# A gated linear attention and an MLP mixer on one core: transposes of one batch element moved from the matrix engine to DMA, relu rows written whole, constants spread over engines, and a new written order

## The chip, the cores and the metric

The kernel runs on one core of a Trainium2 chip. A core has a matrix engine (PE), a vector engine (DVE), a scalar engine (ACT), a general engine (POOL) and an engine that here only issues transfers (SP). Each of them works through its own list of instructions in order and waits on semaphores for the others. Transfers (DMA) are issued by SP and POOL and carried out by 16 DMA engines; those issued by POOL are one queue of their own. The metric is the device time of one run in microseconds (us); lower is better.

## The reference

For each of 4 batch elements (b) and 8 heads a state of 48 x 48 is carried over 768 steps: it decays by a gate per row and takes up an outer product; the output is the query times the state. The outputs of the heads side by side are the rows x of 768 x 384, which go through a mixer over tokens and one over channels.

```python
f = 1.0 / (1.0 + np.exp(-f_logit))
for t in range(S):
    state = f[:, :, t, :, None] * state + np.einsum('bhd,bhe->bhde', k[:, :, t], v[:, :, t])
    y[:, :, t] = np.einsum('bhd,bhde->bhe', q[:, :, t], state)
...
xt = x.transpose(0, 2, 1)
h = np.maximum(xt @ w_tok1, 0.0) @ w_tok2
u = x + h.transpose(0, 2, 1)
h2 = np.maximum(u @ w_ch1, 0.0) @ w_ch2
return (u + h2).astype(np.float32)
```

## The kernel before

The 768 steps are cut into 6 chunks of 128 (c = 0 to 5). For a chunk, ACT makes the logarithms of the gates (`exp`, `ln`), DVE or POOL their low halves (`lo`, L374, L396), PE sums them with a triangle of ones (`sums`, L456, L457, L607, L610), ACT turns the sums into factors (`G`, `Gi`), DVE multiplies q and k with them (`gated`, L485, L629), PE transposes both (`turn`, L495, L636), and PE forms the `scores` (L408, L668), which DVE masks while it reads them from PSUM (`masked`, L536, L698). `parts` (L424, L657) are the outer products of a chunk. The state is carried from chunk to chunk by two DVE operations: `tsum` (L547, L728) adds the parts, and `state` (L549, L730) multiplies by the decay. `spread` (L344 on ACT, L348 on POOL) copies the state as bf16 into a block-diagonal tile for the next chunk, and `y` (L556, L560, L736) is the chunk's output, which leaves PSUM as `x_bf` and `x_nat`. Batch 0 works on its chunks in pairs (function `pair`).

The mixer of a batch element (function `mixer`) is: `tok1` (L750, 12 matmuls in two row tiles, rt 0 and 1) and a relu copy `h1T` (L757); `tok2` (L766) for six token tiles; `u` (L782) and its bf16 copy `u_bf`; the transposes of `u_bf` into `uT`; `ch1` (L819, 24 groups of 3 matmuls) with relu copies `zT`; `ch2` (L838, 6 token tiles with 12 matmuls each, in three blocks of four); `sum` (L844) and `store` (L848). `uT` is made in one of two ways. For batch elements in `UTURN` (2 and 3 before), SP issues two transposing transfers of three token tiles each (L795). For the others, PE makes 3 transposes of 128x128 for each of six token tiles (L804), and DVE or ACT copies each tile out of PSUM.

The queue of POOL holds, besides its arithmetic, all loads of q, k, v, of the gates f of batches 1 to 3 and of the weights (L264, L270); f of batch 0, the row `glast` of each chunk's decay (L476), some transposes and the stores are SP's.

What is done in which order on which engine isn't found by a scheduler at build time: every operation has a number in the order in which it is made in the code, and the string `ORDER` lists the numbers as they are to be issued. A letter behind a number chooses the engine (D for DVE, A for ACT, G for POOL) where an operation allows several, the digits behind a colon choose its PSUM banks, and `z3` stands for three filler matmuls of 512 columns on ones (L870), whose results are not used. Waits follow from the data; each engine takes its part of the list strictly in order. The constants (masks, zeros for padding, ones) are made by `memset` (L277) and `once` at the head of the list, before all on DVE but one.

Of the kernel before, what the change touches and what calls it, by code (L numbers as in the profile page):

```python
# [18 lines left out]
UTURN = (2, 3)  # L19
# [8 lines left out]
POOLED = ()  # L28
LOADS0F = [('f', (0, 2)), ('f', (2, 4)), ('f', (4, 6))]
# [5 lines left out]
32 33 10 5 34 15 21 9 8 22 13 11 0 1 36 24 27 2 49 3 6 35 12 14 20 23 25 26 50 28 7 37 51 52D 54 53D 38 17 z13 105:0  # L35
55 39 19 58 56D 100:1 42 57D 107 29 102 40 z1 137:2 30 106 104 142:3 101 110 43 108 59 103 109 31 119:0:1 18 143 60G
114:4 139 125 111:5 4 61D 144 115 112 41 141 180:0 113A 116D 127G 147 44 138 130 151:4 146 117:5:6 140 181 152 62 121
175:2 126A 131 120 118:5:1 177 176 122 z2 148:6 153A z1 149 123 132G 156:1:2 45 145 182 124:5:4 162 183 178 150A 133G
184 179 47 z3 186:0 163 128A 134 169 155:6:1 135A 185 46 187 159 129A 189:2 188A 208:3 160 190 165G 154:1:5 64 191A
216:6 157 209 67 158 136A z3 193:2:5 164A 217 66 198 192:4:1 170 z1 161:0:2 63 196 195 197 z6 166 194:4 171A 172G 341  # L40
173 200 199:5:1 167A 201 174D 202A 203G 204 210 347 218 71 205D 206 338 211 219 207D 342 212 220 339 213 343G 221 214D
215A 222A 223D 232:3 344 168D 228:4 340G 233 348 229 240 234 224:0 345 241 68 230 244 225 243A 236 252:6 226 242A
250:7 349G 237 245 253D 251A 360:5 231 239A 248:6 346G 256:7 362 249D 368:4 238D 257A 272:6 65 246A 235 280:2 273A 227
254:3 363 396:7 281D 404:0 255A 364 247D 258:6 370 259A 262:2 74 361 270:1 263D 350 69 266:6 369 16 284:2 73 399 264:5
285D 400 260:3 72 271D 265A 302:2 267A 373 300:1 353 70 365 371 374:6 301D 354 48 366:5 372 375D 303A 306:1 261A 75
286:2 398 307D 296:3 367D 287A 355G 378:1 397 377:2 407 381 376:7 76 389 408 304:4 380 276:1 78 305A 388 274:7 405 387
383G 282:4 382A 351 79 278:2 379 283A 294:6 406 401 77 288:5 352D 295A 290:0 275A 409 402:6 277A 289D 291A 384:7 403D
292:1 386A 410:0 279A 390 293D 393:5 297A 392G 298:2 80 395A 411D 433:3 299A 394D 412:1 391G 436 413:4 385D 81 414:5
435 437 416 268:2 434 471:7 417 464:3 269A 424 441:1 472 328:2 425 313:0 415 418 323:4 426 420G 438 421:6 419G 324 82
427 423A 442 430:5 422A 84 325 432D 431A 465 443 439:6 83 326 473 444 314 440A 88 449:4 428A 445:1 452 86 429A 315  # L50
446D 466 453 447:4 448:5 454A 455G 451 467 85 329 450 474 318:4 87 459 456:6 460 319 457A 458D 461:5 316 468 475 462D
308:6 589 356 469 476 320 590 470D 586 477D 330 463D 587 493:7 598 321 481:5 588G 592 331 478:3 595 484:4 479 89 490:0
596 309 482 591D 483A 333:1 485 599 310 494 480A 486G 491 334 495G 597D 604:5 97 600D 487:3 605 496:0 500:7 606 94
498:4 497D 612:2 501D 492A 335 499D 614 488 593 510:4 609 615 530:3 594G 336 613 506:7 311 522:0 511A 93 601 617 610:2
523A 508:4 90 607 640:6 509D 608 518:0 641 91 611D 616 618:4 507A 516:1 531D 489A 92 519A 619D 648:5 504:3 517A 502:7
98 505D 643 620:0 503D 621:1 823 644 622:3 632 96 642 524:7 649 623 534:1 95 650 624 526:6 544:2 357 535D 527A 514:0
631 824 528:6 525A 515D 820 628:4 645 536:7 529A 630D 677:1 545A 646:6 625 537A 546:2 633 651 627G 647D 678 358 532:7
652 629A 653 540:0 626A 533D 547A 656:3 634 541A 658:4 680 654:2 661 659 602 636G 512:0 681 635A 99 520:7 679 662
637:5 513A 660 603G 554:1 655A 670 550:0 682 664G 556:6 639A 663G 521A 657:4 638A 693:3 668 555A 665:7 685:5 832 669
715:2 557 686 551D 687 683:4 667D 666A 708:5 688 829 538:0 671 821 558 539D 673A 822G 833 674:7 696 559 826 689:0 359  # L60
684A 716 548:3 690D 542:6 675D 676A 838:1 825D 543A 709 692:7 672A 549D 691:6 830 704 710 827 571:3 695 561:7 694 711
717 703 845:6 566:4 847 697 839 699G 700:0 846 831G 718 567 701D 841 848 562 698G 842 840 849 572 835 843 332 702D
705:1 327 552:6 706A 707D 317 712 719 828D 553A 844 576:0 720 713 573 721A 714D 872:2 574 722:5 875 737:6 850 731:3
876 738 734:1 851 563 723 739A 735 724A 577 732 736A 581:1 564 733G 834D 728:3 741 582 729 725:7 730A 568 726 874 583
727A 569 836 740 854:3 584 853:4:7 852:5:6 864 879:1 578 855 880 881 784:4 863 873 780:6 579 882 766:2 857 877 772:0
858G 865 907:1 878 773A 770:7 785A 774:0 767A 771D 760:4 859A 312 781D 910 786:7 322 761D 869:6 866 787A 762:4 856
868A 867G 775A 756:2 884 860:5 757A 744:0 885 908 778:7 745D 862A 886:2:3 837D 861A 911 888:0 763A 776:5 883 891 909
890 782:4 777A 892 750:1 779A 900 894G 768:5 783D 751A 893G 752:0 871A 889 914:4 753A 912 742:1 916 870D 895:0 769A
748:3 915 913 746:5 749A 887:4:6 897A 747D 921:7 337 758:2 898 575 788:5 899 759A 936:6 896A 810:3 789D 743A 917 943:0
904:5 919:1:4 918 905D 944 811 922 945 901 937 570 812 924 903A 902G 923 580 938 946 925 764:7 927G 754:1 765A 800:4  # L70
906A 755D 926A 920:5:7 939 932 795:1 931 928:2 801 929D 933:7 947 940 934A 935D 802 948 941 796 949A 942A 790:0 930A
959:6 965:5 950:2 966 962:7 797 967A 963 815:5 960 964G 951 961A 791 952A 969 816 956:6 953:7 957 805:2 565 798 958G
792 954 813 806 955G 803 817 968 793 807 1000:3 1004:7 1016:1 1005A 994:6 1001A 1017D 1002:7 818 1010:1 1003A 819
1014:5 1011D 794 986:7 1015D 799 976:1 987A 585 974:5 996:7 975D 982:3 808 980:5 995D 983A 809 1008:2 981D 560 998:6
977D 984:3 997D 999A 988:1 985A 972:6 989D 978:3 1009D 973A 970:1 1012:2 971A 990:6 1013D 1048:1 1006:7 991A 979A
1033:5 1007A 1038:3 1043:6 1034 1039 1023:7 1018:0 992:2 1049 1044 993A 1050 1040 1051 1052 1028:2 1041 1045 1042 1024
804 1035 814 1025 1036 1029 1046 1026 1047 1019 1027 1030 1037 1020 1031 1032 1021 1022
# [68 lines left out]
def kernel(  # L146
# [126 lines left out]
    def once(name, engine, fn, make, own, need=()):  # L273
        return add(("once", name), engine, fn, make=make, need=need, kind=("fix", own, own))
# [629 lines left out]
```

## Time and profile before

| what | us |
|---|---|
| median of 3 timed runs (lowest, highest) | 173.81 (173.71, 174.67) |
| span of the profiled execution, first to last instruction | 172.8 |
| PE busy | 164.4 |
| DVE busy | 129.1 |
| ACT busy | 109.7 |
| POOL busy | 78.0 |

The profiled execution's own time is known as its span; what lies around the span (start and end of the program) is taken as the difference between the median and the span, 173.81 - 172.8 = 1.0 us. Busy times are unions of an engine's instructions. The page cuts the span into 40 slices of 4.3 us and gives a digit of busy share for each; "PEclk" is the clock that PE was granted, "DMA" the mean busy share of the DMA engines. A row of the groups names source line, engine, operation, result and operand, shape and count, then busy time, mean duration in ns, and the idle time just before with its releaser. A row of the chain gives start, length, engine, tile and line of a piece of the work that ended last.

### The profile page before, as it was taken

The numbers are of one execution on the slowest core, as the hardware profiler recorded it, in microseconds if no ns is written. First come the engines' busy times: TensorE is split into PE (matmuls) and PEld (weight loads), VectorE is DVE, ScalarE is ACT, GpSimd is POOL, SyncE is SP. The second block draws the span as 40 slices with busy tenths as digits, with TensorE's granted clock in tenths as the row PEclk, the third lists the DMA queues.
The fourth block names the chain that finished last, engine by engine and source line by source line (L and its number), as shares of the span: only waits on it lengthen the run. The fifth ranks groups of instructions, "written<-read, shape, count | busy, mean of one in ns | idle before, by whom it ended". The sixth has DMA issues, their size and how long they took to land.

```text
span 172.8 us, 4455 instructions
## 1 busy us (share of the span) xinstructions
PE 164.4 (95%) x1758; PEld 103.6 (60%) x1762; DVE 129.1 (75%) x287; ACT 109.7 (64%) x246; POOL 78.0 (45%) x102
## 2 busy tenths in 40 slices
PE   6889998999999999999999999999999999999991
PEld 2465755566676666676667566666565656656660
DVE  6989996978997789989969859887786355581132
ACT  3997938999893656799999685479933430444100
POOL 2999846998566893799663330010101012000000
PEclk9999999999999999999999999999999999999999
DMA  5999999999997998999999995638155006250054
GB/s 146 217 169 175 246 210 210 157 122 129 197 134 154 182 109 197 133 60 114 108 135 69 63 141 135 144 81 157 32 154 154 1 19 163 89 188 0 2 200 168
DMA packets 89573, 22.74 MB, mean 132 GB/s; under 512 B 82288, under 2 KB 88736, under 8 KB 89552
## 3 DMA queue, kind: packets, MB, share of 16 engines
q0 software_dynamic: 69600, 13.77, 91.7%
q1 hardware_dynamic: 19952, 8.69, 19.6%
q8 instruction: 14, 0.23, 0.6%
q14 instruction: 7, 0.06, 0.1%
HBM read 25.17 MB, written 4.72 MB: 173 GB/s over the span
## 4 chain that ended last, share of the span: by engine, by line
PE 75%; ACT 8%; DVE 5%; issue 1%; DVEq 0%
PE ps L838 26%; PE ps L819 23%; PE ps L750 4%; PE ps L766 4%; PE ps L408 3%; ACT zT L352 2%; PE ps L495 2%; PE ps L456 2%; PE ps L560 2%; PE ps L457 1%; ACT L L367 1%; PE ps L870 1%; PE ps L424 1%; PE ps L804 1%; PE ps L556 1%
## 5 line engine op out<-in xcount | busy, mean ns | idle before, releaser
L838 PE MATMUL ps<-w_ch,zT 128*128 128x384 bf16 (+2 forms) x300 | 52.9, 319 | 0.0
L819 PE MATMUL ps<-uT,w_ch 128*128 128x384 bf16 x288 | 52.4, 326 | 0.3 <-ACT GG L468 0.2
L352 ACT ACTIVATE zT<-ps 128x384 bf16<-128x384 f32 x61 | 28.2, 493 | 19.6 <-PE ps L819 14.6
L838 PEld LDWEIGHTS <-zT 128*128 128x128 bf16 x300 | 28.4, 98 | 17.4 <-issue 0.2
L819 PEld LDWEIGHTS <-w_ch 128*128 128x128 bf16 x288 | 26.9, 97 | 17.0 <-issue 0.7
L354 DVE TENSOR_SCALAR zT<-ps 128x384 bf16<-128x384 f32 x35 | 18.9, 554 | 10.4 <-PE ps L819 8.9
L536 DVE TENSOR_TENSOR AmT<-ps,tri_bf 128x512 bf16<-128x512 f32 x36 | 23.1, 683 | 2.3 <-PE ps L408 2.1
L348 POOL CAST state_bd<-state 48x192 bf16<-48x192 f32 x24 | 9.0, 376 | 34.6 <-DVE state L549 22.2
L844 DVE TENSOR_TENSOR x_nat<-x_nat,ps 128x384 f32<-128x384 f32 (+2 forms) x25 | 12.8, 534 | 10.3 <-PE ps L838 9.8
L264 POOL DMA_DIRECT2D qk_sb<-in_q_dram x16 | 15.9, 1000 | 0.8 <-issue 0.8
L264 POOL DMA_DIRECT2D qk_sb<-in_k_dram x16 | 15.7, 983 | 0.3 <-issue 0.3
L264 POOL DMA_DIRECT2D v_sb<-in_v_dram x16 | 15.7, 983 | 0.1
L782 DVE TENSOR_TENSOR x_nat<-x_nat,ps 128x384 f32<-128x384 f32 x21 | 10.8, 549 | 4.2 <-PE ps L766 4.1
L750 PE MATMUL ps<-x_bf,w_tok 128*128 128x384 bf16 x48 | 13.2, 326 | 0.3 <-DVE zT L698 0.2
L348 POOL CAST u_bf<-x_nat 128x384 bf16<-128x384 f32 x6 | 3.0, 506 | 20.7 <-DVE x_nat L782 20.7
L374 POOL TENSOR_TENSOR Llo<-L 128x384 bf16<-128x384 f32 x10 | 8.2, 826 | 6.4 <-ACT L L367 6.3
L485 DVE TENSOR_TENSOR qk<-qk_sb,GG 128x768 bf16<-128x768 bf16 x18 | 9.9, 555 | 1.4 <-ACT GG L468 1.4
L870 PE MATMUL ps<-x_nat 128*128 128x512 bf16 x26 | 8.7, 460 | 2.0 <-DVE x_nat L279 1.5
L466 ACT ACTIVATE GG<-ps 128x384 bf16<-128x384 f32 x18 | 8.7, 492 | 2.5 <-PE ps L457 2.3
L344 ACT ACTIVATE x_bf<-ps 128x384 bf16<-128x384 f32 x13 | 6.5, 499 | 5.9 <-PE ps L560 5.0
L766 PE MATMUL ps<-h1T,w_tok 128*128 128x384 bf16 x48 | 9.4, 326 | 0.8 <-ACT h1T L352 0.6
L468 ACT ACTIVATE GG<-ps 128x384 bf16<-128x384 f32 x18 | 8.9, 492 | 1.8 <-PE ps L457 1.6
(96 smaller groups left out, 266.4 us busy)
## 6 DMA issues: line engine op xcount, KB each, us to landing
out_dram<-x_nat SPq DMA_DIRECT2D x23, 192.0 KB, 2.2
f_sb<-in_f_logit_dram POOLq DMA_DIRECT2D x3, 1152.0 KB, 11.1
f_sb<-in_f_logit_dram SPq DMA_DIRECT2D x3, 384.0 KB, 4.2
w_ch<-in_moe_w_ch_dram POOLq DMA_DIRECT2D x2, 576.0 KB, 13.2
qk_sb<-in_q_dram POOLq DMA_DIRECT2D x12, 96.0 KB, 6.6
qk_sb<-in_k_dram POOLq DMA_DIRECT2D x12, 96.0 KB, 5.6
v_sb<-in_v_dram POOLq DMA_DIRECT2D x12, 96.0 KB, 4.5
w_ch<-in_moe_w_ch_dram POOLq DMA_DIRECT2D x1, 1152.0 KB, 10.0
```

What stands on the lines that cost most here:

```text
L264: lambda eng=eng, into=into, of=of: eng.dma_start(out=into, in_=of),
L348: nc.gpsimd.tensor_copy(out_, in_)
L352: nc.scalar.activation(out_, in_, AF.Relu, bias=0.0, scale=1.0)
L354: nc.vector.tensor_scalar(out_, in_, 0.0, None, ALU.max)
L536: add(("masked", b, c, p), DVE, lambda half=half, made=made: nc.vector.tensor_tensor(half, made(), tb4, ALU.mult), need=["tri_bf"], make=[ ...
L750: add(("tok1", b, rt, kt), PE, lambda rt=rt, kt=kt, pm=pm: nc.tensor.matmul(banks[pm.at][:, 0:DM], lhsT=w_tok1[:, kt, rt * 128:(rt + 1) * ...
L766: nc.tensor.matmul(banks[pm.at][:, 0:DM], lhsT=w_tok2[:, kt, tt * 128:(tt + 1) * 128], rhs=h1T[:, kt, :], start=(kt == 0 and not held), st ...
L782: nc.vector.tensor_tensor(to, un, banks[pm.at][:, 0:DM], ALU.add)
L819: nc.tensor.matmul(banks[pm.at][:, 0:384].rearrange("p (n t) -> p n t", t=128), lhsT=w[:, kt, c0:c0 + 128], rhs=uT[:, rows3, kt, :], start ...
L838: nc.tensor.matmul(banks[pm.at][:, 0:n1 - n0], lhsT=zT[:, kt, tt * 128:(tt + 1) * 128], rhs=w_ch2[:, kt, n0:n1], start=(kt == 0), stop=(kt ...
L844: add(("sum", b, tt, n0), DVE, lambda un=un, pm=pm, n=n1 - n0: nc.vector.tensor_tensor(un, un, banks[pm.at][:, 0:n], ALU.add), make=[("x_n ...
L870: nc.tensor.matmul(banks[NBANK - 1][0:rows, 0:cols], lhsT=steady[:, 0:rows], rhs=steady[:, 0:cols], start=True, stop=True)
```

## The change

Five things are changed.

1. `UTURN` becomes (1, 2, 3): the 18 PE transposes of batch 1's `u_bf` and their six copies out of PSUM give way to two transposing transfers that SP issues.
2. `h1T` of batch 0 is copied in two whole rows (384 columns), not in four halves.
3. The constants may be made by DVE or POOL (`memset`) and by DVE or ACT (`copied`). In the new list 11 of the memsets are POOL's and 2 copies are ACT's.
4. The `state` multiplication of a chunk may run on POOL; in the new list 11 of 20 do, three of them in batch 0.
5. `ORDER` is a new list for all engines. It has 23 filler matmuls where the old one had 30 (13 of them at the head in both), other engines for some copies, other PSUM banks, and another order of the loads.

The diff, without the two lists and with the moved helper `copy_on` left out:

```diff
-UTURN = (2, 3)
+UTURN = (1, 2, 3)
...
+HALVES = False
+STATES = (DVE, POOL,)
...
     def memset(name, tl, value, make, own):
-        once(name, DVE, lambda: nc.vector.memset(tl, value), make, own)
+        op = once(name, (DVE, POOL), None, make, own)
+        op.fn = lambda: (nc.gpsimd if op.engine == POOL else nc.vector).memset(tl, value)
+
+    def copied(name, out_, in_, make, own, need):
+        op = once(name, (DVE, ACT), None, make, own, need)
+        op.fn = lambda: copy_on(op.engine, out_, in_)
...
-    once("ident0", DVE, lambda: nc.vector.tensor_copy(ident[:, 0:1], tri_bf[:, 0:1]), ["ident"], 70, ["tri_bf"])
+    copied("ident0", ident[:, 0:1], tri_bf[:, 0:1], ["ident"], 70, ["tri_bf"])
...
-            once(f"inc2{n}", DVE, lambda rows=rows: nc.vector.tensor_copy(inc2[rows, rows], tri_bf[rows, rows]), ["inc2"], 130,
-                 ["tri_bf"])
...
+            copied(f"inc2{n}", inc2[rows, rows], tri_bf[rows, rows], ["inc2"], 130, ["tri_bf"])
+            copied(f"pmask0{n}", pmask[0][rows], tri_bf[rows, rows].unsqueeze(2).broadcast_to((64, 64, 2)), [("pmask", 0)], 200,
+                   ["tri_bf"])
...
-                add(("state", b, c), DVE, lambda: nc.vector.tensor_tensor(state, tsum, gb, ALU.mult),
-                    need=["tsum", ("glast", g4)], make=["state"], kind=small)
+                decayed(b, c, gb, ("glast", g4))
...
+    def decayed(b, c, gb, key):
+        op = add(("state", b, c), STATES, None, need=["tsum", key], make=["state"], kind=("el", HP * D, True, 1))
+        op.fn = lambda: (nc.gpsimd if op.engine == POOL else nc.vector).tensor_tensor(state, tsum, gb, ALU.mult)
...
-            half = DM // 2 if b == 0 else DM
+            half = DM // 2 if b == 0 and HALVES else DM
```

What the new list does at the places that the prediction speaks of:

- **Head.** POOL makes tri, one zero tile and five paddings before its first load; DVE has fewer constants ahead of its first `lo`, and all six `lo` of batch 0 are DVE's.
- **Loads.** POOL issues the gates f of batch 1 ahead of v of the last chunk pair and of the token weights; the set of transfers ahead of `w_tok2` stays the same.
- **First mixer.** All 12 `tok1` of batch 0 stand behind the last `y`. The six of rt 0 and one of rt 1 come first, the other five of rt 1 last. Of the twelve `tok2` matmuls, the first four need only rt 0. `h1T` of rt 0 is DVE's and of rt 1 is ACT's. One `sums` of batch 1 (two matmuls of 384) now stands in the attention of batch 0.
- **Batch 1's `uT`.** The last of the first three `u_bf` hangs on the `tok2` of token tile 2, behind which PE has six blocks of four `ch2` matmuls and three `tok2` pairs until the first `ch1` of batch 1. On POOL's queue f of batch 2 and seven loads of its v, q and k stand ahead of that point; only one `state` among them waits for anything.

More of the change, by code (lines that the diff above doesn't have):

```diff
@@ L40 @@
[L40 to L54, printed above, removed]
@@ L75 @@
[L75 to L77 removed]
+0G 18G 1 12D 2 11D 24A 21D 20D 32 27D 5G 23A 49 33 8G 17G 50 51 29D 22D 26D 54 10D 13G 7D 14D 3D 25D 6G 36 34 55 28 35
+37 30D 52D 58 39 z13 53D 9G 105:0 100:1 106 15D 56D 101 57D 142:2 102 103 38 40 108 137:1 107 31D 110 109 59 143 19G 144
@@ L271, in load_w, with copy_on @@
             make=[name], kind=("load", 900, 1024, size))
+    def copy_on(eng, out_, in_):
+        if eng == ACT:
+            nc.scalar.activation(out_, in_, AF.Copy, bias=0.0, scale=1.0)
+        elif eng == DVE:
+            nc.vector.tensor_copy(out_, in_)
+        else:
+            nc.gpsimd.tensor_copy(out_, in_)
     def once(name, engine, fn, make, own, need=()):
@@ L340, in blk @@
         return ap3.rearrange("t (hp par) dd -> t hp (par dd)", par=2)
-    def copy_on(eng, out_, in_):
-        if eng == ACT:
-            nc.scalar.activation(out_, in_, AF.Copy, bias=0.0, scale=1.0)
-        elif eng == DVE:
-            nc.vector.tensor_copy(out_, in_)
-        else:
-            nc.gpsimd.tensor_copy(out_, in_)
     def relu(eng, out_, in_):
@@ L729, in pair @@
                         need=["state"], make=["tsum"], bank=p_d[k], kind=small)
-                    add(("state", 0, c), DVE, lambda gb=gb: nc.vector.tensor_tensor(state, tsum, gb, ALU.mult),
-                        need=["tsum", ("gpair", i2)], make=["state"], kind=small)
+                    decayed(0, c, gb, ("gpair", i2))
                 spread(0, c)
```

72 lines of the change are left out of this document (42 added, 30 removed).

## The prediction

> **What bounds the kernel now.** I read the page's first two parts, then busy time by stretch, then the chain of waits around the seam between the first two stretches.
>
> ```profile
> span 172.8 us, 4455 instructions
> ...
> PE 164.4 (95%) x1758; PEld 103.6 (60%) x1762; DVE 129.1 (75%) x287; ACT 109.7 (64%) x246; POOL 78.0 (45%) x102
> ...
> PE   6889998999999999999999999999999999999991
> DVE  6989996978997789989969859887786355581132
> ...
> DMA  5999999999997998999999995638155006250054
> ```
>
> PE looks like the bound everywhere, but fillers count as busy. The stretches below tell more; the columns are stretch, length, then busy time and count of PE, weight loads, DVE, ACT and POOL.
>
> ```profile
> 5.90:28.80 22.90, 20.80 (x437) 13.79 (x439) 20.47 (x50) 17.74 (x38) 18.29 (x24) 1.00 1.54 197
> 28.80:32.70 3.90, 3.12 (x22) 1.70 (x21) 2.77 (x8) 3.44 (x10) 3.53 (x6) 1.00 1.67 183
> 32.70:169.30 136.60, 136.01 (x1291) 86.39 (x1289) 101.24 (x208) 85.66 (x197) 53.39 (x67) 1.00 1.07 117
> ```
>
> From 32.7 us on PE is busy 136.0 of 136.6 us: there every PE instruction costs its time, and every wait of PE is new time. In the attention of batch 0 (5.9 to 28.8 us) DVE has 20.5 of 22.9 us with its waits for PE and transfers in the rest, and PE's 20.8 us hold 17 fillers: there DVE leads. So the sum has two parts: when the first `tok2` can stream, and what PE must do after it.
>
> ```profile
> 28.21 0.98 PE ps L750 x5
> 29.21 0.37 DVE h1T L354
> 29.61 0.56 ACT h1T L352 x2
> 30.19 0.37 DVE h1T L354
> 30.60 1.46 PE ps L766 x8
> ```
>
> The seam: `tok1` ends at 29.19, four half copies of `h1T` follow one another, and `tok2` streams only from 30.60 (two of its matmuls went before). 1.4 us for 0.33 us of PE work.
>
> **The change part by part. The front.** DVE's work there, by group (result and operand, count, then busy us and mean ns):
>
> ```profile
> L698 DVE TENSOR_TENSOR zT<-ps,x_nat 128x512 bf16<-128x512 f32 x12 | 7.7, 682 | 0.4 <-PE ps L668 0.4
> ...
> L396 DVE TENSOR_TENSOR Llo<-L 128x384 bf16<-128x384 f32 x5 | 2.5, 528 | 0.0
> L730 DVE TENSOR_TENSOR state<-tsum,gpair 128x192 f32<-128x192 f32 x4 | 1.4, 354 | 0.2
> ...
> L323 DVE COPY x_nat<-x_nat 64x64 bf16<-64x64 bf16 x2 | 1.0, 492 | 0.1
> ...
> L277 DVE MEMSET state_bd<- 128x192 uint32 x2 | 0.4, 218 | 0.2
> ...
> L321 DVE COPY x_nat<-x_nat 128x128 bf16<-128x128 bf16 x1 | 0.3, 345 | 0.0
> ```
>
> And five rows of the timeline (start, length, engine, line, operation):
>
> ```profile
> 5.14 0.94 ACT L383 ACTIVATE L<-f_sb 128x384 f32<-128x384 f32 x2
> ...
> 5.94 0.50 DVE L396 TENSOR_TENSOR Llo<-L 128x384 bf16<-128x384 f32 x1
> ...
> 10.97 0.83 POOL L396 TENSOR_TENSOR Llo<-L 128x384 bf16<-128x384 f32 x1 [0.23 <-ACT L L383]
> ...
> 11.07 0.78 DVE L323 COPY x_nat<-x_nat 64x64 bf16<-64x64 bf16 x1
> ...
> 27.26 1.54 DVE L346 CAST x_bf<-ps 128x384 bf16<-128x384 f32 x3
> ```
>
> Between the first `lo` and the last `x_bf`, the new list takes from DVE: two zero tiles (2 x 0.218), the copy of L321 (0.345) and one of L323 (two in 0.98 us, one of them 0.78, so the other 0.20), which now stand before the first `lo` or on POOL: 1.0 us; and three of the four L730 (3 x 0.354 = 1.06). It adds the sixth `lo` (0.53). Masks and `x_bf` keep their number (12 and 3). Net: 1.0 + 1.06 - 0.53 = 1.5 us; 2.1, if the other L323 falls from 0.78 to 0.20. The first `lo` started at 5.94, behind DVE's constants; its logarithm, the first of two in 0.94 us from 5.14 on, is done by about 5.6. With fewer constants ahead `lo` can start then: 0.3 us more. So the last `x_bf` of batch 0 comes about 1.8 us sooner, at 27.0 instead of 28.8 (27.26 + 1.54). From there, six `tok1` remain by the new list instead of two: four more at 0.163 us (four matmuls as wide in 0.65 us, L838 below) are 0.65 us back. The seam itself shrinks: rt 0's relu (one row of 0.55 us on DVE) lies under the five last `tok1`, the first four `tok2` (0.65 us) lie over rt 1's relu on ACT (0.5 us), and some 0.3 us of wait is left instead of 1.1: 0.8 us won. Together 1.8 - 0.65 + 0.8 = 2.0 us (1.95): where `tok2` streamed from 30.60 with two done, as good as 30.3, it streams from about 28.3.
>
> Fillers stand only where PE waits, so the seven that go are inside this sum and not added to it. Transfers allow it: the set ahead of `w_tok2` is the same as before, POOL's queue is full from the start, and `w_tok2`, issued at 16.7, landed 10.4 us later, at 27.0.
>
> ```profile
> L270 POOL DMA_DIRECT2D w_tok<-in_moe_w_tok_dram x1: 713/713/713, 16.7 to 16.7; - x1
> ...
> DMA to landing us min/median/max: 10.4/10.4/10.4
> ```
>
> Nearly all `tok2` need it at once, so the front can win at most 3.3 us (30.3 - 27.0); at the low end it wins nothing, if ACT (17.7 us busy, and with gates of batch 1 moved ahead of its `h1T`) takes the lead. I take 2.0.
>
> The moved constants on POOL: no row of before has a POOL memset of such a size. From below, nothing; from above, 0.83 us each, the row of POOL's `lo` of 384 columns. They stand before its first load, in time in which POOL had waited for DVE's triangle; each us by which they outlast it moves all loads and that floor by as much, which the range holds. The `state` on POOL: bounded by 0.35 (DVE's row) and 0.83 (twice the columns); about 0.45, 0.1 us more per step of the state's chain, hidden behind DVE's masks.
>
> **After the first `tok2`.** Rows of the chain for what leaves PE, and for the time of batch 1's `tok2`:
>
> ```profile
> 35.11 0.17 PE ps L456
> 35.28 0.16 PE ps L457
> ...
> 66.27 1.62 PE ps L766 x10
> ...
> 71.16 0.50 PE ps L804 x9
> 71.99 0.65 PE ps L838 x4
> ```
>
> 18 transposes at 0.50 / 9 = 55.6 ns are 1.0 us, all on the bound. One `sums` (0.33 us) now runs in the front, where PE has room: 0.3 us. The six copies of `uT` leave DVE and ACT, which are not the bound there: 0. `ch1` and `ch2` keep their counts.
>
> What comes instead is a wait. PE's list has, between the `tok2` of token tile 2 of batch 1 and the first `ch1` on its `uT`, six blocks of `ch2` (0.65) and three pairs of `tok2` (0.33): 4.9 us. In that time the chain `u` on DVE, `u_bf` on ACT, transfer must end:
>
> ```profile
> L782 DVE TENSOR_TENSOR x_nat<-x_nat,ps 128x384 f32<-128x384 f32 x21 | 10.8, 549 | 4.2 <-PE ps L766 4.1
> ...
> L344 ACT ACTIVATE u_bf<-x_nat 128x384 bf16<-128x384 f32 x12 | 6.1, 522 | 6.0 <-DVE x_nat L782 6.0
> ...
> uT<-u_bf SPq DMA_TRANSPOSE x4, 2.8
> ...
> f_sb<-in_f_logit_dram POOLq DMA_DIRECT2D x3, 1152.0 KB, 11.1
> ...
> w_ch<-in_moe_w_ch_dram POOLq DMA_DIRECT2D x1, 1152.0 KB, 10.0
> ```
>
> 0.55 + 0.52 + 2.8 = 3.9 us: hidden, with 1.0 us to spare. But the four transfers behind the 2.8 ran after 108 us, in slices of the DMA line with 6 tenths or less. Those of batch 1 fall with its `tok2` at about 66 us, in slices of 8 and 9 tenths, and POOL's list has f of batch 2 (11.1 us to land) and seven loads ahead of them. How a transposing transfer fares there no row tells. The nearest is SP's small transfer of `glast`, by its landing in two stretches, 100 to 106 us and 35 to 44 us:
>
> ```profile
> DMA to landing us min/median/max: 2.0/2.0/2.7
> ...
> DMA to landing us min/median/max: 3.5/4.3/6.1
> ```
>
> It takes 1.5 to 4.1 us more among loads, 2.3 in the middle. For `uT` that gives 4.3 to 6.9 us, against 3.8 that are hidden: a wait of 0.5 to 3.1 us, and in proportion (2.8 x 6.1 / 2.0 = 8.5) up to 4.7; from below, 0. I take the least busy end plus some, 0.9 us, since by its list POOL has only loads of q, k and v left in its queue then, as at the 3.5. The second transfer has about the same slack, and a wait for the first gives it more. For `glast` of batch 1, which now stands nearer to its `state`, and for `w_ch2` (10.0 us to land, issued later), I add 0.2 us; 0 to 2 is open.
>
> **Sum.** -2.0 (front) - 1.0 (transposes) - 0.3 (`sums`) + 0.9 + 0.2 (waits) = -2.2 us. The tail after the last `ch2` keeps its shape. The profiled span of 172.8 becomes 170.6; with the 1.0 us around the span that lie between it and the median of 173.8, **171.6 us**.
>
> **Rivals.** First, slower: **the transposes land late among the loads.** Each is a transfer of many small pieces that shares the 16 DMA engines with POOL's full queue. If `uT` takes three times its 2.8 us, as `glast` did at its worst, PE stands 4.7 us instead of 0.9: -2.2 - 0.9 + 4.7 = +1.6, 175.4 us. It decides from a landing of some 7 us on, where the wait eats the 3.3 us won and no gain is left. For it: the 8 and 9 of the DMA line at 66 us and the 6.1. Against it: the 3.5, and a queue that should have drained to small loads by then.
>
> Second, **the front doesn't get shorter**: ACT, which gets four operations of batch 1 ahead of rt 1's `h1T`, or the landing of `w_tok1` and `w_tok2`, takes DVE's place. Then -1.3 + 1.1 = -0.2: 173.6 us.
>
> Third, **POOL's new arithmetic holds DVE up.** The two copies of L323 speak for it: 0.20 us the one, 0.78 the other, which ran beside POOL's `lo` (10.97 to 11.80). If two of the three POOL `state` of the front each block DVE for their 0.45 us, 0.9 of the 2.0 us is lost: 172.5. Against it: much of DVE's work there are masks that read PSUM (L698, 7.7 of 20.5 us), and the state's product comes right behind a `tsum`, with masks next in DVE's list. The Trainium skill, page "SBUF — State Buffer", section "Who interferes with whom", has a rule that speaks against this part of the change: DVE and POOL share one pair of ports as an exclusive lock; a DVE copy in its fast modes, or a DVE operation with two SBUF inputs, and a POOL operation that reads SBUF keep each other out for a whole instruction. By that rule, the 0.78 agrees.
>
> That the change doesn't do what it says is excluded: the new list has six PE `ut` and six transfers, as said.
>
> **How the numbers follow.** Forecast 0.52 (its own range 169.8 to 172.9: -4.0, with the front at 2.7 and no waits, to -0.9, with the front at 1.0 and 1.4 of waits); late transposes 0.21; front unchanged 0.15; POOL against DVE 0.12. The measurement can tell about 0.5% from no change, 0.9 us: under 172.9 is faster, over 174.7 slower. Forecast and POOL's rival are faster (0.64), the unchanged front is the same (0.15), the late transposes are slower (0.21). For 8 in 10 the range runs from 169.8 up to 175.2, which leaves out about half of the late transposes and a little below.
>
> **What would show it.** Right: the first `tok2` streams by 28.3 us; DVE's busy time between the first `lo` and the last `x_bf` down by 1.5 to 2 us; L804 gone from the stretch after 60 us, and the first `ch1` of batch 1 waiting for a transfer by about 1 us. Wrong: that wait at 3 us or more and SP's transposes landing after over 6; a first `tok2` at 30; waits of PE for `glast`'s `state` or for `w_ch2`.

## The result and the profile after

The changed kernel takes 183.8 us (median of four runs, 181.5 to 185.9) where the kernel before takes 173.9 on the same chip: slower, ratio 1.045 [1.037, 1.053]. The ratio leaves out the two slowest of the four runs; the medians of all runs stand at 1.057. The profiled execution is the slowest of the four, 185.9 us with a span of 184.1; its clock was 0.969 on the mean, that of the fastest 0.991.

The page of the changed kernel, first two parts, rows as in the prediction's first fence:

```profile
span 184.1 us, 4400 instructions
...
PE 166.1 (90%) x1734; PEld 104.2 (57%) x1737; DVE 127.3 (69%) x267; ACT 105.3 (57%) x232; POOL 90.5 (49%) x128
...
PE   6999689895969999879679999999999999999992
...
PEclk9999999996996999999978999999999999999998
```

PE has new holes (the digits below 9 up to the 21st slice of 4.6 us, some 97 us), and the clock dips three times. From 98 us on PE runs as before. What ends the holes is in the chain of waits (start, length, piece):

```profile
37.85 4.46 DMA glast<-grow
...
42.44 0.36 DVE state L548
...
43.57 1.12 PE ps L825 x3
...
48.90 5.66 DMA glast<-grow
...
54.69 0.52 POOL state L576
...
55.65 0.34 PE ps L756
...
74.26 5.01 DMA uT<-u_bf
...
79.31 0.82 PE ps L825 x4
...
84.42 7.45 DMA glast<-grow
...
91.99 0.06 DVE state L548
...
93.00 0.65 PE ps L825 x3
```

Three of the four holes end with a gate row, `glast`: 2 KB that SP moves from `grow` so that the state of a chunk can be multiplied. It takes 4.5 to 7.5 us to land; PE's first instruction behind each comes 1.1 to 1.3 us after the landing, through DVE or POOL. The third hole ends with the first transposing transfer of batch 1. The changed kernel by stretch (length, busy time and count of PE, PEld, DVE, ACT and POOL, then granted clock, DMA share and GB/s):

```profile
43.60:46.30 2.70, 2.70 (x19) 1.60 (x19) 1.58 (x3) 1.45 (x4) 2.70 (x4) 0.50 0.88 46
...
55.60:62.00 6.40, 6.36 (x49) 4.00 (x50) 5.12 (x10) 3.34 (x8) 5.18 (x7) 0.73 1.54 80
...
93.00:98.00 5.00, 5.00 (x22) 2.46 (x22) 4.42 (x9) 2.73 (x7) 4.05 (x4) 0.66 0.45 25
98.00:180.40 82.40, 81.79 (x759) 52.12 (x756) 54.54 (x108) 40.06 (x91) 20.32 (x32) 1.00 0.74 103
```

Behind each gate row's hole PE runs for some time at a lower clock: busy, and yet half as fast. If the gaps between the starts of PE's groups of matmuls beyond their pitch are added up over the trace (no view shows this sum), PE lost 7.5 us before and 21.2 after, 13.7 more; what PE has to do fell by 2.5 (18 transposes, seven fillers). The difference, 11.2, is that of the spans (184.1 - 172.8 = 11.3). With the slow clock behind them, the holes at 43, 56 and 93 us make 3.6, 3.4 and 4.6 us of it, those of the two `uT` 2.35.

### The profile page after: what moved, and what is told of

Same layout as the page of the kernel before. It is cut to its first block, busy times and chain, and to the rows that moved or that the text cites. A ratio compares the mean times of both kernels' runs of the same rounds, so it can differ in the third digit from the quotient of the medians.

```text
span 184.1 us, 4400 instructions
## 1 busy us (share of the span) xinstructions
PE 166.1 (90%) x1734; PEld 104.2 (57%) x1737; DVE 127.3 (69%) x267; ACT 105.3 (57%) x232; POOL 90.5 (49%) x128
## 4 chain that ended last, share of the span: by engine, by line
PE 59%; DMA 15%; POOL 10%; DVE 7%; issue 4%; ACT 3%; SPq 0%; DVEq 0%; POOLq 0%
PE ps L825 20%; PE ps L844 19%; DMA glast<-grow 10%; PE ps L756 4%; POOL qk_sb L265 3%; DMA uT<-u_bf 3%; DMA qkT<-qk 3%; PE ps L772 2%; PE ps L563 2%; POOL state_bd L280 2%; PE ps L559 2%; PE ps L499 1%; PE ps L412 1%; POOL v_sb L265 1%; DVE AmT L540 1%
## 5 line engine op out<-in xcount | busy, mean ns | idle before, releaser
L825 PE MATMUL ps<-uT,w_ch 128*128 128x384 bf16 x288 | 56.7, 340 | 7.0 <-DVE AmT L540 2.7
L356 ACT ACTIVATE zT<-ps 128x384 bf16<-128x384 f32 x47 | 21.9, 494 | 23.8 <-PE ps L825 23.3
L358 DVE TENSOR_SCALAR zT<-ps 128x384 bf16<-128x384 f32 x49 | 25.7, 551 | 12.7 <-PE ps L825 9.4
L850 DVE TENSOR_TENSOR x_nat<-x_nat,ps 128x384 f32<-128x384 f32 (+2 forms) x25 | 13.0, 533 | 10.4 <-PE ps L844 8.8
L280 POOL CAST state_bd<-state 48x192 bf16<-48x192 f32 x26 | 10.2, 393 | 18.5 <-DVE state L548 9.9
L576 POOL TENSOR_TENSOR state<-tsum,glast 128x192 f32<-128x192 f32 x8 | 5.0, 622 | 20.4 <-DVE tsum L551 16.4
L756 PE MATMUL ps<-x_bf,w_tok 128*128 128x384 bf16 x48 | 11.7, 333 | 1.9 <-DVE tsum L551 1.9
L280 POOL CAST u_bf<-x_nat 128x384 bf16<-128x384 f32 x8 | 3.9, 505 | 16.4 <-DVE x_nat L788 16.4
L378 POOL TENSOR_TENSOR Llo<-L 128x384 bf16<-128x384 f32 x11 | 9.4, 862 | 5.3 <-ACT L L371 5.0
L276 ACT ACTIVATE state_bd<-state 48x192 bf16<-48x192 f32 x14 | 5.0, 360 | 12.1 <-POOL state L576 5.4
L472 ACT ACTIVATE GG<-ps 128x384 bf16<-128x384 f32 x18 | 8.8, 487 | 3.5 <-PE ps L461 3.4
```

Source lines behind the costliest of these rows:

```text
L276: nc.scalar.activation(out_, in_, AF.Copy, bias=0.0, scale=1.0)
L280: nc.gpsimd.tensor_copy(out_, in_)
L356: nc.scalar.activation(out_, in_, AF.Relu, bias=0.0, scale=1.0)
L358: nc.vector.tensor_scalar(out_, in_, 0.0, None, ALU.max)
L756: add(("tok1", b, rt, kt), PE, lambda rt=rt, kt=kt, pm=pm: nc.tensor.matmul(banks[pm.at][:, 0:DM], lhsT=w_tok1[:, kt, rt * 128:(rt + 1) * ...
L825: nc.tensor.matmul(banks[pm.at][:, 0:384].rearrange("p (n t) -> p n t", t=128), lhsT=w[:, kt, c0:c0 + 128], rhs=uT[:, rows3, kt, :], start ...
```

## The experiments

Theory G: the new list issues the gate rows too late for what they take among loads. Theory T: the transposing transfers of batch 1 cost the time, and the gate rows are their victims. Lists are shown by operations; `after` and `before` in brackets say from which kernel an experiment starts.

**All gate rows of batches 1 and 2 by PE and ACT** (after):

```diff
-TOTALS = [(0, 0), (0, 1), (0, 2), (0, 3), (0, 4), (0, 5)]
+TOTALS = [(b, c) for b in range(3) for c in range(6)]
 ORDER, for each of these chunks:
-ACT grow b c ... SP glast b c
+ACT glast b c
```

> The changed kernel, in which the last rows of the gates of batches 1 and 2 no longer go through SP's transfers: four matmuls of two rows and a copy on ACT make glast there, as batch 0 does already; two zero tiles more at the start on DVE, ten times four small matmuls more on PE (some 0.5 us). All else, the transposes of batch 1 by transfer among it, stays. Theory G (late gate rows cost the time: 3.6 + 3.4 + 4.6 us of PE's lost time, each wait over 2 us with a stretch of half clock behind it): 172 to 175 us, and only the wait for uT of about 2 us left. Theory T (the transposing transfers of batch 1 cost it, gate rows are their victims): 180 us or more, since those transfers stay.

176.5 us, ratio 1.014 [1.011, 1.016]. Of the waits only the second uT's stays (2.4 us at 79.4 us). With the sums of the last chunks, which get them too, it is 96 small matmuls that take 2.65 us from start to start, not the 0.5 of the expectation. G was nearer, T is out for this list: the transfers stayed and 7.3 us went.

**Fillers in the waits** (after):

```diff
+PE z10 (bank 3)  before ch1 0 1 0
+PE z9  (bank 7)  before tok1 1 1 0
+PE z8  (bank 4)  before ch1 1 0 8
+PE z12 (bank 1)  before ch1 1 1 8
```

> The changed kernel with 39 filler matmuls of 512 columns, whose results nobody uses, put into PE's list ahead of the four instructions that wait longest (10, 9, 8 and 12 of them, each group a little shorter than the wait that it fills). The waits stay; only PE is busy in them. If the half clock behind each long wait comes from PE standing still (theory G's second half), the three stretches of about 3.4 us at half clock go and the time falls by some 5 us, to 178 to 179 us. If the clock falls for another reason, or the waits alone cost the time: 183 to 184 us.

The first group writes over a bank that still holds the sums of chunk 3 of batch 1, so that what follows from these is computed from other numbers; the times of instructions don't hang on it. What PE was granted:

```profile
PEclk9999999999999999999999999999999999999999
```

That is the clock row of its page. But the time is 184.5 us, ratio 1.061 [1.054, 1.067], no less than without fillers. So the standing still does make the slow clock, and the 5 us that the expectation put on the slow clock aren't there. A smaller price isn't excluded: the two profiled executions, the fastest of four here and the slowest of four there, differ by 2.3 us in span (181.8 for 184.1). The landings hint why so little is won: w_ch2 landed at 55.60 instead of 55.48 us, and chunk 2's gate row, issued 1.4 us sooner, at 53.8 instead of 54.6, although PE had kept its clock: the next hole ends when a transfer lands, whatever PE did before it. The second half of theory G, 5 us for the clock, fell.

**f of batch 3 later** (after):

```diff
-POOL load f 3 ... state 2 1
+POOL state 2 1, load f 3
 ACT exp 3 5, exp 3 1 behind exp 3 2
```

> The changed kernel with one transfer moved: the load of f of batch 3 (1152 KB) is issued behind POOL's state of batch 2, chunk pair 1, instead of ahead of the gate rows of batch 2; the logarithm and exponentials that read it move accordingly. If a large transfer in flight is what makes the gate row of batch 2 take 7.45 us to land, that row lands in 2 to 3 us, the wait at 92 us and its half clock go: some 4.5 us less, 179 us. If the row is late only because it is issued late: within 1 us of 183.8.

188.9 us, ratio 1.082 [1.076, 1.088]: slower by 5, which neither side expected. Yet the rows did what was asked. SP's issues between 84 and 87 us or so (count, KB each, median us to landing), first this kernel, then the changed one:

```profile
glast<-grow SPq DMA_DIRECT2D x3, 2.0 KB, 2.4
```

```profile
glast<-grow SPq DMA_DIRECT2D x3, 2.0 KB, 6.4
```

Issued from 84.8 to 86.8 us, instead of 84.4 to 86.4, three rows land in 2.1 to 3.6 us, instead of 6.0 to 7.5, since no 1152 KB are in flight. The time was lost elsewhere. This kernel's waits and POOL's timeline:

```profile
PE ps L558 <- POOL state_bd L279: 3.8, 1, 3.8
```

```profile
92.39 0.50 POOL L575 TENSOR_TENSOR state<-tsum,glast 128x192 f32<-128x192 f32 x1 [0.23 <-ACT state_bd L275]
92.90 2.29 POOL L264 DMA_DIRECT2D f_sb<-in_f_logit_dram  x1
...
103.40 2.21 POOL L264 DMA_DIRECT2D qk_sb<-in_k_dram  x1 [4.30 <-issue]
105.65 0.73 POOL L279 CAST state_bd<-state 48x192 bf16<-48x192 f32 x2
```

Between the product at 92.39 and the two spreads of its result at 105.65 POOL's list now has f of batch 3 and other loads, and POOL stands 4.3 us ahead of one of them, until 0.35 us after f has landed at 103.05. PE waits 3.8 us for the spreads.

**Transposes by transfer alone** (before):

```diff
-UTURN = (2, 3)
+UTURN = (1, 2, 3)
 ORDER
-PE ut 1 0..5, DVE/ACT uT 1 0..5
+SP ut 1 0 behind u_bf 1 0..2, SP ut 1 1 behind u_bf 1 3..5
```

> The kernel before, with one part of the change alone: u of batch 1 turned by two SP transfers, its 18 PE transposes and six copies left out; the rest of the list as it was, gate rows with their old distance. By the prediction's working (1.0 us of transposes less, 0.9 us of wait): 173.8 us, same. By theory T: 180 us or more. By theory G with transfers that land in 5 to 6 us: waits of 2 to 4 us less the 1.0, perhaps with a stretch of half clock, 175 to 178 us.

187.0 us (183.3 to 188.4) against 174.0 (173.7 to 174.4): 13 us slower by the medians, 9.6 by the fastest run of each, for 1.0 us of transposes left out. Its chain of waits, and two stretches with the clock:

```profile
70.22 6.45 DMA uT<-u_bf
...
76.72 3.06 PE ps L817 x9
...
82.12 7.68 DMA uT<-u_bf
...
89.84 3.38 PE ps L817 x10
```

```profile
76.60:80.20 3.60, 3.48 (x18) 1.97 (x19) 0.00 (x0) 1.29 (x3) 3.60 (x5) 0.56 2.00 104
...
89.80:93.40 3.60, 3.56 (x12) 1.70 (x13) 1.16 (x2) 1.42 (x4) 0.00 (x0) 0.50 0.54 20
```

The transfers land in 6.5 and 7.7 us, PE waits 4.3 and 5.5 us, and runs 3.6 us at about half clock behind each. In the old list `ch1` of batch 1 stands close behind its transposes; the new list puts other work between, and there the same two transfers cost 2.35. So both theories name a real price, and which of them is paid is a matter of the list.

**Transposes of batch 1 back on PE** (after):

```diff
-UTURN = (1, 2, 3)
+UTURN = (2, 3)
 ORDER
-SP ut 1 0, SP ut 1 1
+PE ut 1 0..5 and ACT/DVE uT 1 0..5, behind each u_bf
```

> The changed kernel with one part undone: u of batch 1 is turned on PE again (18 transposes, six copies, no transfer), in the new list; the gate rows stay as they are. Theory G (late gate rows alone make the waits at 43, 56 and 92 us): the wait for uT (2.3 us) goes, 1.0 us of PE work comes, the other three waits stay: 182 to 184 us. Theory T (the transposing transfers cost the time, or delay the gate rows): 174 to 176 us, with gate rows that land in 2 to 3 us.

185.6 us, ratio 1.060 [1.053, 1.066]. Without a single transposing transfer in batch 1 the time stays, and so do the waits for gate rows, in this kernel's table of waits (us in total, times, longest):

```profile
POOL state L576 <- DMA glast<-grow: 10.8, 2, 6.4
DVE state L548 <- DMA glast<-grow: 2.9, 2, 2.3
```

The rows of batch 1 land in 3.9 to 6.4 us. The transposes were put back clumsily, all but one through one PSUM bank: around them, from 79 to 86 us, PE has five waits of 0.5 to 1.5 us, 4.5 in all, while the hole at 93 us shrank to 0.5. Even without these five the time would be some 181 us (185.6 - 4.5), far from theory T's 174 to 176, and the holes at 43 and 56 us are as before (waits of 2.0 and 2.3 us for 2.2 and 1.9): the two gate rows behind them are no victims of the transposes.

**Four gate rows by PE, f of batch 3 behind POOL's last `lo` of batch 2** (after), and two variants of it:

```diff
-TOTALS = [(0, 0), (0, 1), (0, 2), (0, 3), (0, 4), (0, 5)]
+TOTALS = [(0, 0), (0, 1), (0, 2), (0, 3), (0, 4), (0, 5), (1, 0), (1, 2), (2, 0), (2, 1)]
 ORDER, the four new rows as in the first experiment, and
-POOL load f 3, load q 2 4, lo 2 5
+POOL load q 2 4, lo 2 5, load f 3
```

> The changed kernel with the two causes taken away at least cost: only the four gate rows that PE waited for or would wait for next (chunks 0 and 2 of batch 1, chunks 0 and 1 of batch 2) are made by PE and ACT (32 small matmuls, 0.9 us by their pitch), and the load of f of batch 3 is issued behind POOL's last lo of batch 2, so that the second uT and the rows of batch 2 have no 1152 KB in flight beside them. From the run with all gate rows by PE, 176.5: 64 small matmuls less (1.8 us), a uT wait of 2.4 us that falls to under 1: 172.5 to 174 us. If the second uT is late for a reason other than f of batch 3: 174.5 to 176 us.

181.8 us (179.3 to 183.1), ratio 1.027 [1.019, 1.036]: slower than with all rows by PE. The second uT still took 6.2 us, with f of batch 3 not yet issued, and the moved load is paid for at about 100 us, in POOL's waits:

```profile
POOL v_sb L265 <- ACT f_sb L371: 3.5, 1, 3.5
```

The row names ACT's exponential of f as what came last, but the load of v needs nothing of it. POOL begins this load at 101.88, 0.35 us after q of batch 3 (576 KB) has landed at 101.53, and it stood another 2.1 us before the load of k, which begins at 93.88, 0.33 us after f has landed at 93.55. In the next run POOL stands before the same two loads and begins them 0.33 and 0.35 us after the same two landings, the second 1.3 us after ACT's last instruction. So what POOL stands for is the landing of an earlier big load: with f moved behind, f, q and k of batch 3 follow one another closely, and the `spread` and `lo` behind them on POOL come late (PE waits 1.6 us for the one and 1.6 us for the other). The same with the transposes back on PE:

> As the kernel with four gate rows by PE and the later load, and u of batch 1 turned on PE besides, so no transfer of batch 1 is left to wait for. If the transfers of batch 1 still cost waits there, this is faster by up to 1.5 us; if they are hidden, it is slower by the 1.0 us of 18 transposes. Theory T wants it at 172 or less, theory G at 173 to 175 us.

185.3 us, ratio 1.058 [1.052, 1.064]; none of the expectations had that. PE lost some 12 us more than before there, much of it between 72 and 84 us, around the transposes, with waits of 0.4 to 1.5 us. It is the same clumsy way back to PE, and so the run tells nothing on the transfers.

And with the three state products of batch 0 back on DVE (`POOL state 0 1..3` becomes `DVE state 0 1..3`):

> As the kernel with four gate rows by PE and the later load, and the three state products of batch 0 that the change gave to POOL (0.51 to 0.64 us each) back on DVE (0.35 us). If POOL's queue of loads and slower products is what keeps the front long, the first tok2 comes at 28.7 to 29.2 us instead of 29.6 and the time falls by 0.4 to 0.9 us; if DVE leads the front, as the prediction had it, the front gets 0.5 to 1.0 us longer.

180.9 us, ratio 1.029 [1.022, 1.036], the same. The front tells more: `tok1` and the first `tok2` in the chain of this kernel, then of the one with four gate rows:

```profile
29.37 1.95 PE ps L757 x12
31.32 0.92 PE ps L773 x5
```

```profile
28.01 1.95 PE ps L757 x12
29.96 0.91 PE ps L773 x5
```

With the products on DVE the front is 1.4 us longer. The change's move to POOL is a gain there, and DVE does lead without it; the later waits swallow it.

**Gate rows earlier** (after), the same instructions in another order:

```diff
-ACT G 1 0, Gi 1 0, ..., grow 1 0     SP glast 1 0, glast 1 1 (at 37.9, 38.5)
+ACT grow 1 0, G 1 0, Gi 1 0, grow 1 2  SP glast 1 1, glast 1 0, glast 1 2 (at 31.1, 35.3, 37.1)
 grow 1 3 behind Gi 1 2; grow 2 1 ahead of Gi 2 1; grow 2 0 ahead of G 2 0
 each SP glast directly behind its grow
```

> The changed kernel with the same instructions; only the places of gate rows in ACT's and SP's lists differ: each of the rows of chunks 0 to 3 of batch 1 and of chunks 0, 1 and 3 of batch 2 is made as the first reader of its sums or soon after, and its transfer is issued at once instead of behind a later one (chunk 0 of batch 1 at 34.4 instead of 37.85 us, chunk 2 at 36.5 instead of 48.9, chunk 0 of batch 2 at 83 instead of 84.4). No transfer is taken away, and each lands in the same 4 to 6 us or so. Theory G in its narrower form (the list issues the rows too late for a landing of 4 to 7 us): the waits at 43 and 56 us go (7 us with the clock behind them), that at 92 us shrinks by about 1.4: 174.5 to 177 us. If the rows then land later still, because the loads ahead of them are what they wait for and not their own issue: 180 us or more.

177.8 us, ratio 1.022 [1.017, 1.027]: 6.0 of the 9.9 us are back by the medians, about half of the loss by the ratios (1.045 and 1.022), with nothing but places in the list. Slightly over the range. PE's holes at 56 and 93 us are gone. At 43 us 0.6 us stay, behind chunk 0's row, and 0.7 us at 38 us are new and no row's:

```profile
PE ps L824 <- ACT zT L355: 0.7, 1, 0.7
```

Two `grow` now stand ahead of this relu copy on ACT, so it ends at 38.3 us and frees its PSUM bank late: early rows have a price of their own. Chunk 0's row was issued 2.5 us sooner and landed only 0.2 us sooner than in the changed kernel. POOL's timeline of this kernel, and the issues around 34 to 35.5 us (KB each, us to landing):

```profile
34.04 0.75 POOL L270 DMA_DIRECT2D w_ch<-in_moe_w_ch_dram  x1
34.77 0.93 POOL L264 DMA_DIRECT2D qk_sb<-in_k_dram  x1
```

```profile
w_ch<-in_moe_w_ch_dram POOLq DMA_DIRECT2D x1, 576.0 KB, 7.7
...
glast<-grow SPq DMA_DIRECT2D x1, 2.0 KB, 6.8
```

Half of w_ch1, issued at 34.04, lands at 41.78; the row, issued at 35.33, at 42.09; the load of k issued between them at 42.8. The small transfer lands 0.3 us behind the half, and 0.7 us ahead of a load that was issued before it.

**Early rows, f of batch 3 later, spreads on ACT** (after):

```diff
 as the run before, and
+POOL load f 3 behind lo 2 5
-POOL spread 2 1, spread 2 2
+ACT spread 2 1 (behind Gi 2 3), spread 2 2
+DVE u 1 5 ahead of sum 0 5; ACT u_bf 1 5 ahead of exp 2 4
```

> As the kernel with early gate rows, and: the load of f of batch 3 behind POOL's last lo of batch 2; the four spreads of batch 2, chunks 1 and 2, on ACT instead of behind POOL's 576 KB loads; u of token tile 5 of batch 1 one place earlier on DVE and its u_bf two places earlier on ACT, so that the second uT is issued some 0.6 us sooner. If waits for small transfers and for POOL's queue are all that the change cost, and its 2.5 us less of PE work are real, this beats the kernel before: 171.5 to 173.5 us. If the second uT still lands in 6 us or more with only loads of q, k and v beside it: one wait of 1.5 to 2 us stays, 173 to 175 us.

In this kernel the spreads of chunk 1 copy the state before its product is made, so batch 2 is computed with an older state there. 181.3 us, ratio 1.040 [1.035, 1.044]: f late costs again (POOL stands 3.7 us before the load of k, until f has landed, and 3.5 before that of v, until q has), and the second uT, issued 0.7 us sooner, took 6.95 us. Both sides missed.

**What the rows wait for, put to use** (after, early rows), and its converse (before):

```diff
 early rows, and
-POOL load w_ch1 1, load k 1 2, load q 1 3, load k 1 3
+POOL load k 1 2, load q 1 3, load k 1 3, load w_ch1 1
-PE ch1 1: first and second half mixed
+PE ch1 1: twelve of the first half, then twelve of the second
 zT of batch 1 in the order of their ch1, some on the other of ACT and DVE
+DVE u 1 5 ahead of sum 0 5; ACT u_bf 1 5 ahead of exp 2 4
-POOL load w_tok2, load k 1 1, spread 0 1 0, state 0 2, spread 0 2 0
+POOL spread 0 1 0, load w_tok2, state 0 2, spread 0 2 0, load k 1 1
```

> As the kernel with early gate rows, and three moves that follow from what a small SP transfer seems to wait for, the loads issued ahead of it: the half of w_ch1 that was issued at 34.0 us goes behind three loads of q and k (chunk 0's gate row, issued at 35.3, should then land at 38 to 39 instead of 42.1); the twelve ch1 of batch 1's first half go ahead of the twelve of its second half, and u and u_bf of token tile 5 go one or two places up, so that the second uT has some 2 us more; in the front the loads of w_tok2 and of k's chunk 1 go behind POOL's spread and product of batch 0, chunks 1 and 2 (0.9 us of the state's chain). From 177.8: the waits at 38 and 43 us (1.6), that for the second uT (2.2) and 0.9 of the front go: 172.5 to 174.5 us, as fast as the kernel before. If a small transfer's landing doesn't follow the loads ahead of it, the gate row still lands at 42 and the time stays above 175.5.

175.7 us, ratio 1.0054 [1.0018, 1.0090] over 12 runs: the best of all, a little over the expected 172.5 to 174.5, and still no faster than the kernel before. The row of chunk 0 did as forecast, by the issue around 35.1 us:

```profile
glast<-grow SPq DMA_DIRECT2D x1, 2.0 KB, 2.8
```

It was issued at 35.14, as the w_ch1 half hadn't been yet, and landed at 37.98 instead of 42.09. The wait of 0.7 us at 38 us, which is ACT's, stays. The wait of 2.2 us for the second uT is gone: it landed at 79.59, and the 0.4 us that PE stands at 80.5 end with a relu copy of DVE. But the first uT, issued with its old distance, took 4.9 us instead of 3.9, and PE now loses 1.7 us on it. The front's 0.9 us didn't come: POOL's spread, moved forward, ran beside DVE's products of q and k and took 1.27 us instead of 0.34, so that `tok2` starts at 29.8.

```diff
 before's ORDER
-POOL load v 1 3, load k 1 2, load q 1 3, load k 1 3, load q 1 2, load w_ch2
+POOL load w_ch2, load v 1 3, load k 1 2, load q 1 3, load k 1 3, load q 1 2
```

> The kernel before with one load moved: w_ch2 (1152 KB) is issued at about 34.2 us, ahead of the last load of v and four loads of q and k, instead of at 38.5 behind them; nothing else differs. If a small SP transfer lands with the loads issued ahead of it, chunk 0's gate row, issued at 35.5, lands at 43 to 45 instead of 39.1 us, past the 42.9 at which its product starts, and PE waits: 1 to 5 us slower, 175 to 179. If only the issue counts, it lands at 39 to 40 and the time stays at 173.5 to 174.5.

176.9 us, ratio 1.012 [1.004, 1.019]. The row, issued at 36.0, took 6.1 us instead of 3.5 and landed at 42.05: late as forecast, by a load that it has nothing to do with, though a little ahead of the 44.4 at which the load landed. But that wasn't what PE waited for. PE's longest new wait, 1.5 us for the transposes of chunk 2, hangs on q, in the table of waits:

```profile
DVE qk L484 <- DMA qk_sb<-in_q_dram: 2.1, 1, 2.1
```

So the run bears out the landing, and not the price put on it.

## Why the prediction was wrong, step by step

- **The gate rows, +0.2 us with 0 to 2 open: this step failed, and most of the loss is here.** The rows' lateness was named, and the landing among loads was known from the profile (3.5 to 6.1 us), but the step priced only a row "nearer to its state". Nobody counted for each row its issue, its landing and the time at which its product is due. The new list makes `grow` of chunk 0 as the last reader of the sums, sends chunk 1's row behind it, and issues chunk 2's row 10.4 us later than before (48.9 for 38.5). Measured: 11.6 of the 13.7 us that PE newly lost in the profiled execution, the slow clock behind the holes included; 6.0 us back by the medians when the rows are merely issued earlier (ratio 1.022 for 1.045), 7.3 when they need no transfer (1.014).
- **The wait for uT, +0.9 us: right in kind, 2.35 us in size.** The landings were 5.0 and 6.0 us in the changed kernel; the forecast's price came from the least busy end of what the rows allowed, with the argument that POOL would have only loads of q, k and v in flight. It had, and that is enough for 6 us. The step had the transfer leave 1.07 us after its last `tok2`; it left 1.6 us after, since DVE had three `u` one behind the other, and that is 0.5 of the 1.8 us lost on the first. The first rival's mechanism is real, and alone in the old list it costs 9.6 us or more; in the new list it isn't what decides.
- **The front, -2.0 us: -0.7.** In the chain of the changed kernel the first `tok2` streams at 29.59, not at 28.3:

```profile
16.24 0.52 POOL state L576
...
16.82 0.34 POOL state_bd L280
...
17.26 0.77 POOL w_tok L271
18.03 0.58 POOL qk_sb L265
...
18.97 0.34 POOL state_bd L280
...
19.39 0.50 POOL state L576
...
27.64 1.95 PE ps L756 x12
29.59 0.49 PE ps L772 x3
```

  The last `x_bf` came at 28.23 instead of 28.80, not at 27.0, and the parts of this 0.57 can be told: DVE's first `lo` started 0.34 us sooner (5.60), as said; from there to the last `x_bf` DVE was busy 19.57 us instead of 20.43, 0.86 less where 1.5 were forecast (0.53 of the lack is a copy that the step left out: the new list gives DVE `turned` of q, 1.21 us, where it had that of k, 0.68); and it waited 3.06 us instead of 2.43, of which 0.7 is for POOL's product at 19.39. The chain here goes through POOL: products and spreads, between them the issues of loads, 1.35 us of them in this cut. The part behind the last `x_bf` held: `tok2` follows `tok1` at once, 1.36 us after `x_bf` instead of 1.5, as in the sum. The prediction's second rival had looked for the new lead in ACT or the weights; by the chain it was POOL's queue, though the run that moved two loads behind POOL's links won nothing there.
- **POOL's products, a rival at 172.5:** they were slower than estimated (0.50 to 0.53 us for 0.45), but as a whole they shorten the front by 1.4 us, as the run with three of them on DVE shows. What the third rival feared, one engine holding up the other, happened in both directions, and not by the products. POOL is held: a spread beside DVE's products of q and k takes 0.80 us, elsewhere 0.34, by the two engines' timelines in the changed kernel:

```profile
13.91 0.89 DVE L636 TENSOR_TENSOR qk<-qk_sb,GG 128x384 bf16<-128x384 bf16 x3
```

```profile
14.20 0.80 POOL L280 CAST state_bd<-state 48x192 bf16<-48x192 f32 x1
```

  By the rule of the Trainium skill quoted in the prediction (page "SBUF — State Buffer", section "Who interferes with whom") either of the two engines may keep the other out; this row agrees, with POOL as the one that waits. DVE is held too, beside the issue of a load on POOL:

```profile
9.50 0.72 DVE L278 COPY x_nat<-x_nat 64x64 bf16<-64x64 bf16 x1
```

```profile
9.27 0.92 POOL L265 DMA_DIRECT2D qk_sb<-in_q_dram  x1
```

  In the changed kernel and in nine of the ten that start from it this copy begins between 9.50 and 9.90 us and ends at 10.22 to 10.24, some 0.03 us after the issue has ended; in the tenth it begins at 9.45 and takes 0.20 us. So a copy of 0.20 us is held for up to 0.5. That the issue holds it is read from these edges; no run moved the one or the other alone.
- **The 18 transposes, -1.0 us, and `sums`:** PE has 24 instructions less on the page (1734 for 1758; 18 transposes and seven fillers are 25, and the record of one can be missing), and its work fell; this part held. What moving the one `sums` won by itself no run shows.
- **Not in the sum:** the lower clock behind each long wait. The fillers took it away and the median didn't fall, so its absence from the sum isn't what made the forecast fail.

What stays open: 3.9 of the 9.9 us are left with early rows. About 2.9 us of PE's lost time there are the waits for uT at 74 and 81 us, 0.8 the row behind w_ch1 and 0.9 the late relu copy at 38 us; the best version got back 2.1 us by the medians. Why it isn't faster than the kernel before, with 1.0 us less for PE to do, is only counted (some 3 us more lost than before, 1.7 of them for the first uT and 0.9 at 38 us), not taken apart by a run.

## What to carry to other kernels

A small transfer on a quiet queue tells nothing of one behind a big load: price it by the landing of what was issued ahead of it, and then move its issue to before the load. When an order is rewritten as a whole, list for every small transfer three times, issue, landing and due, before and after; a list that looks busier on the bound engine can have spent the slack of something that nobody looked at. An engine whose list holds both loads and links of a dependent chain makes the chain wait for each issue, and for what the issue itself waits for, and may be the next lead when another engine is unloaded.

## What the runs showed of the hardware

SP's transfers of 2 KB landed in 1.9 to 2.1 us on a quiet machine and in up to 8.2 among loads, about when the loads issued ahead of them on POOL's queue landed, not by their size:

| kernel | small transfer | landed | big load issued ahead | landed |
|---|---|---|---|---|
| after | `glast`, 37.85 | 42.31 | w_ch1 half, 33.61 | 41.33 |
| after | `glast`, 48.90 | 54.56 | w_ch2, 45.50 | 55.48 |
| after | `glast`, 84.42 | 91.87 | f of batch 3, 82.05 | 92.05 |
| early rows | `glast`, 35.33 | 42.09 | w_ch1 half, 34.04 | 41.78 |
| early rows, w_ch1 behind | `glast`, 35.14 | 37.98 | none (three loads of 96 KB) | 36.6 to 38.5 |
| before, w_ch2 ahead | `glast`, 36.00 | 42.05 | w_ch2, 34.63 | 44.39 |
| transposes alone | `uT`, 82.12 | 89.80 | k of batch 3, 576 KB, 80.31 | 91.36 |

The Trainium skill, page "DMA: Bandwidth & Descriptors", section "Queues, rings and completion order", states two things that bear on this: each DMA engine takes turns between the queues that have work, and the write that counts a semaphore up lands only after every earlier write of that DMA engine, across its queues. By the first alone a transfer on SP's queue would pass POOL's loads; by the second its completion waits for writes ahead of it. The rows above agree with the second, except that four of them land 0.2 to 2.3 us before the big load's own completion; no run here separates the two.

"Issued ahead" goes by the ends of the issues. In the kernel with transposes alone two gate rows were issued while POOL was still at the issue of k (80.31 to 82.58 us), from 80.84 to 81.31 and from 81.43 to 81.95, and landed in 2.5 and 2.1 us; the uT, issued from 82.12 to 83.67, took 7.7. With w_ch1 behind, chunk 2's row was issued from 36.88 to 37.35, the half of w_ch1 until 37.23, and the row took 6.0.

POOL itself stood before a load until an earlier big one had landed: ten times in six kernels (four of the five with f of batch 3 moved twice, the fifth once, and before with w_ch2 ahead once) it stood 1.6 to 4.3 us, and the load began 0.29 to 0.35 us after a load of 576 or 1152 KB had landed. In the changed kernel, where f of batch 3 is issued 14 us ahead of q, it didn't stand there.

Waits of PE of 1.9 to 2.7 us were followed by up to 3.4 us of half clock (0.50 from 43.60 to 46.30), and fillers in the waits removed it. The Trainium skill, page "TensorE: Matmul & The Clock Gate", section "Part 1: The HAM clock gate (the "warmup" mystery)", puts the half clock behind at least one idle window of about 3.4 us; here shorter waits were enough.
